# Two gated long convolutions: tables of 28 channels at once, a shift filter by matmuls on a transposed k, fixed regions instead of pools, and a new order

## The chip, the cores and the metric

The kernel runs on one core of one Trainium2 chip. The metric is the device time of one execution in microseconds (us); of several runs the median counts. A core has five engines with a queue each: PE (matmul), DVE (vector), ACT (scalar, with function tables), POOL (here index patterns) and SP (which issues most of the DMAs). Each engine works through its own queue in order, and semaphores hold an instruction until what it needs is there.

## What is computed

Two branches over L = 2048 steps and D = 448 channels are mixed by a gate. All inputs and the output are bf16.

```python
# branch A (N = 256 modes per channel)
dt = exp(log_dt); A = A_re + 1j*A_im; dB = dt*(B_re + 1j*B_im); C = C_re + 1j*C_im
K[d, l] = sum_n( C[d, n] * exp(dt[d] * A[d, n] * l) * dB[d, n] ).real
a = causal_conv(u, K) + u * Dskip                      # by FFT of length 2L in the reference
# branch B
k_shift[t] = sum_{i<4} k[t - i] * shift_k[:, i]        # 4 taps, per channel
kv = k_shift * v
b = q * (causal_conv(kv, ssm_k) + kv * ssm_D)
# mix
g = sigmoid(sum_d u[:, d] * gate_w[d])
out = g * a + (1 - g) * b
```

In this kernel's inputs u stands in for q.

## The kernel before, in words

Layout. The 448 channels are four groups of 112. An array such as u, v or k lies in SBUF with partition 32g + a for group g and slow time index a (32 of them), and with 64 fast time steps times 112 channels in the free dimension (7168 numbers to a partition). The work goes by quarters H = 0..3 of 28 channels of each group, that is 112 channels at a time.

Convolutions. Each one is a discrete Fourier transform in stages, all by matmul. `spread` (constants Wc, WcK) turns the slow index into frequencies, `transform` (constant s_W) the fast one; both leave PSUM through ACT copies into tiles `zs` of 128x3584. `swapped` makes a second copy with the real and imaginary halves exchanged, by two DMAs of 448 KB on SP. `products` multiplies both copies by the other operand's spectrum (DVE, 3584 wide). `stage_a` (constant R) and `stage_b` (constant G, 1024 matmuls of 28 columns) go back to time, with ACT copies into a tile U between them. `epilogue_B` multiplies by u, `held` keeps a result, `mix` and `epilogue_A` do the gate.

Tables. The kernel K of branch A is the costly part. For each quarter `Tables.chunk` (`levels`, `reals`) makes powers of exp(dt*A) at a few exponents: phases on DVE (80 instructions of 128x224 in the whole kernel, half of them with a quarter turn added), Sin on ACT (40 of 448), magnitudes by Exp (ACT), a multiplication of both (DVE, 36), and a copy with the sign turned (`nc.scalar.mul(..., -1.0)`, ACT, 20). From them `KGen.block(j)` builds, for each of 8 blocks of 14 channels (M = 112 modes and channels in the free dimension), two tables by repeated complex multiplication on DVE: kg_TQ (25 rows, two buffers) and kg_TP (32 rows, one buffer), with kg_P as room for the four products of each complex one. 224 matmuls `pk` of 25x32 for each block sum over the modes, ACT copies the sums to kg_S, `gather` puts them in order of time with selection matmuls (`ga_sel`, 448 in all, and 8 for Dskip), and `spread` with WcK follows.

Shift filter. k is loaded by 16 DMAs in the natural layout with a halo of three steps (`kt`, 128x67x112). For each of 8 groups of 8 steps DVE multiplies by the four taps at once (`kvt`, 128x3584), 64 identity matmuls `ps_v` of 448 columns in all add the four, ACT copies the sums back to kt, and four DVE multiplications by v make kv.

Constants. `Consts.stage_b` makes G by 8 DVE phases of 512 and 16 ACT Sin of 1024, with the mask as Sin's scale.

Buffers. A pool qp of eight slots (`NBQ = 8`) of 128x3584, pools for the natural arrays, three PSUM tiles of two banks and two of one bank for the tables. The tile framework hands out slots in turn, and makes an instruction wait until its buffer is free. ssm_k arrives per quarter in a slot of its own.

Order. The code's calls are recorded by `Listed` and `Order` (lines 119 to 150) and issued in the order of the string ORDER (lines 41 to 107), each instruction held behind the one before it on its engine. That is why every instruction shows as line 144 in the profile: one reads the groups by tile names. The recorded sequence is B0, B1, B2, A0, B3, A1, A2, A3 (kind and quarter), with a block of tables in each step (`step`), and a tail that takes the last block, the mix, and A3 in two halves.

Of the kernel before, what the change touches and what calls it, by code (L numbers as in the profile page):

```python
# [18 lines left out]
PHASE = 6.2831845 / 65536  # L19
QUARTER = 16384.0  # L20
# [5 lines left out]
NBLK = 2 * NQG  # L26
M = 8 * CB
NMODE = 896
Q_LEVELS = (4, 2, 256, 1, 512)
P_LEVELS = (8, 16, 32, 64)  # L30
NR = 16
NQ = 25
EQ_N = 2 + 3 * len(Q_LEVELS)
EP_N = 2 + 3 * len(P_LEVELS) + NR
ENT = EQ_N + EP_N
E_P0 = EQ_N
E_R = EQ_N + 2 + 3 * len(P_LEVELS)
NBQ = 8
NBH = 1

ORDER = (
# [65 lines left out]
)  # L107

def entry_of(e):
    return 2 + 3 * Q_LEVELS.index(e) if e in Q_LEVELS else EQ_N + 2 + 3 * P_LEVELS.index(e)  # L110

# [518 lines left out]
def body(  # L630
# [158 lines left out]
    def kv_cols(H):  # L789
        return lambda c: kvq[H][:, :, c]  # L790
# [205 lines left out]
```

## Time and profile before

| | before |
|---|---|
| runs | 281.84, 285.15, 285.49 us, median 285.15 |
| span of the profiled execution | 282.3 us, 12050 instructions |
| DVE busy | 261.8 us (93%), 540 instructions |
| ACT busy | 250.8 us (89%), 409 instructions |
| PE busy | 213.7 us (76%), 5387 matmuls |
| POOL busy | 12.0 us (4%), 43 instructions |
| DMA | 53380 packets, 21.34 MB; 48720 packets under 512 B |

The profiled execution's own time is its span, 282.3 us, which lies between the lowest and the middle run; the median is 2.85 us above it. The profile's slices are 40 equal parts of the span (7.06 us each), a digit being tenths of busy time. A group of instructions is named by engine, operation, out<-in tile names and shape; behind the count stand the busy time of the group, the mean ns of one, and the idle time before. Stretches by window give the busy time of PE, PEld (weight loads), DVE, ACT and POOL, the TensorE clock granted, the share of DMA and the rate.

### The profile page before, as it was taken

How to read it: one execution, taken by the hardware profiler on the slowest of the kernel's cores; microseconds unless marked ns; L12 is line 12 of the kernel's file. 1: busy time of each engine (PE TensorE's matmuls, PEld its weight loads, DVE VectorE, ACT ScalarE, POOL GpSimd, SP SyncE). 2: the span in 40 equal slices, each digit the busy share in tenths (PEclk: the TensorE clock that was granted, in tenths of full speed). 3: DMA queues.
4: the chain of work that ended last, by engine and by line, in shares of the span. 5: the costliest groups of instructions: out<-in, count | busy, mean ns of one | idle time of the engine just before them, and what ended most of it. 6: DMA issues, size and time to landing. Idle time of an engine off the chain costs nothing.

```text
span 282.3 us, 12050 instructions
## 1 busy us (share of the span) xinstructions
PE 213.7 (76%) x5387; PEld 185.9 (66%) x5387; DVE 261.8 (93%) x540; ACT 250.8 (89%) x409; POOL 12.0 (4%) x43
## 2 busy tenths in 40 slices
PE   0187673776697869888889898879899999979730
PEld 0044243776586768877779787868789887869730
DVE  8999999999999997999999999999968999987950
ACT  5999999999999999999999999999979999948500
POOL 8005000001000001000000000000000000000000
PEclk9999797565888997999999997988979999979995
DMA  6999997590501360240000070015050003430068
GB/s 116 190 182 176 158 168 105 187 175 6 135 2 19 69 115 10 73 107 2 5 2 5 6 181 0 5 22 114 9 128 2 2 5 73 112 88 5 2 126 138
DMA packets 53380, 21.34 MB, mean 76 GB/s; under 512 B 48720, under 2 KB 51664, under 8 KB 53328
## 3 DMA queue, kind: packets, MB, share of 16 engines
q1 hardware_dynamic: 48768, 19.42, 37.2%
q10 hardware_dynamic: 4560, 1.15, 2.2%
q8 instruction: 42, 0.69, 1.1%
q14 instruction: 10, 0.08, 0.1%
HBM read 10.01 MB, written 3.21 MB: 47 GB/s over the span
## 4 chain that ended last, share of the span: by engine, by line
ACT 34%; DVE 30%; PE 21%; issue 5%; DMA 3%; SPq 2%; DVEq 0%
ACT zs L144 11%; PE pk L144 8%; ACT ET L144 8%; DVE kg_P L144 7%; DVE kg_TP L144 5%; PE ps_b L144 4%; ACT zsK L144 4%; ACT U L144 4%; DVE zsS L144 3%; PE ps_c L144 3%; PE ps_a L144 3%; DVE kg_TQ L144 3%; DVE zs L144 2%; DVE kvt L144 2%; DVE ks_ph L144 2%
## 5 line engine op out<-in xcount | busy, mean ns | idle before, releaser
L144 ACT CAST zs<-ps 128x896 bf16<-128x896 f32 x48 | 44.0, 940 | 0.8 <-PE ps L144 0.7
L144 ACT CAST zs<-ps_c 128x1024 bf16<-128x1024 f32 (+1 forms) x48 | 43.4, 933 | 0.0
L144 PE MATMUL pk<-kg_TP,kg_TQ 128*25 128x32 bf16 x1792 | 33.8, 239 | 8.8 <-issue 6.6
L144 PEld LDWEIGHTS <-s_W 128*128 128x128 bf16 x544 | 31.0, 105 | 12.1 <-issue 8.7
L144 PEld LDWEIGHTS <-kg_TQ 128*25 128x25 bf16 x1792 | 28.6, 128 | 12.2 <-issue 8.2
L144 PE MATMUL ps_a<-sa_R,zs 128*128 128x128 bf16 x224 | 34.1, 239 | 3.0 <-ACT zs L144 1.3
L144 DVE TENSOR_TENSOR kg_P<-kg_TQ,ET 128x896 bf16<-128x896 bf16 (+2 forms) x56 | 35.9, 654 | 0.0
L144 PE MATMUL ps<-zs,s_W 128*128 128x112 bf16 x384 | 29.3, 231 | 7.3 <-ACT zs L144 6.2
L144 PE MATMUL ps_a<-sa_R,zsS 128*128 128x128 bf16 x224 | 33.7, 239 | 1.2 <-DVE zsS L144 1.2
L144 PEld LDWEIGHTS <-zsS 128*128 128x128 bf16 x224 | 30.1, 153 | 4.9 <-issue 3.0
L144 ACT CAST U<-ps_a 128x1024 bf16<-128x1024 f32 (+2 forms) x30 | 28.6, 959 | 5.0 <-PE ps_a L144 5.0
L144 PE MATMUL ps_b<-U,sb_G 128*128 128x28 bf16 x1024 | 28.8, 174 | 3.4 <-DVE U L144 1.2
L144 PEld LDWEIGHTS <-zs 128*128 128x128 bf16 x224 | 30.2, 152 | 1.3 <-issue 0.3
L144 PEld LDWEIGHTS <-sb_G 128*128 128x128 bf16 x1024 | 27.8, 96 | 4.3 <-issue 2.3
L144 DVE TENSOR_TENSOR kg_P<-kg_TP,ET 128x1792 bf16<-128x1792 bf16 (+1 forms) x32 | 30.6, 969 | 0.0
L144 DVE TENSOR_TENSOR kg_TQ<-kg_P 128x448 bf16<-128x448 bf16 (+2 forms) x56 | 23.1, 419 | 0.0
L144 PEld LDWEIGHTS <-scratch 128*128 128x128 bf16 x65 | 6.8, 109 | 24.6 <-issue 19.7
L144 ACT ACTIVATE ET<-ks_ph 128x448 bf16<-128x448 int16 x40 | 22.5, 604 | 0.0
L144 ACT CAST zsK<-ps_c 128x384 bf16<-128x384 f32 (+2 forms) x27 | 21.3, 797 | 0.6 <-PE ps_c L144 0.6
L144 DVE TENSOR_TENSOR kg_TP<-kg_P 128x896 bf16<-128x896 bf16 (+2 forms) x40 | 19.7, 503 | 0.2 <-PE pk L144 0.2
L144 PE MATMUL ps_c<-Wc,kv 128*64 128x128 bf16 x224 | 16.6, 303 | 3.9 <-ACT zs L144 3.6
L144 PE MATMUL ps_v<-kvt,scratch 128*128 128x448 bf16 x64 | 16.1, 405 | 4.0 <-ACT kt L144 3.2
(103 smaller groups left out, 463.3 us busy)
## 6 DMA issues: line engine op xcount, KB each, us to landing
zsS<-zs SPq DMA_DIRECT2D x16, 448.0 KB, 5.7
kt<-in_B_k_dram SPq DMA_DIRECT2D x16, 112.0 KB, 4.0
skraw<-in_B_ssm_k_dram SPq DMA_DIRECT2D x16, 112.0 KB, 5.0
vt<-in_B_v_dram SPq DMA_DIRECT2D x4, 448.0 KB, 7.7
uu<-in_A_u_dram SPq DMA_DIRECT2D x4, 448.0 KB, 8.8
xfd<-ks_hold SPq DMA_DIRECT2D x2, 672.0 KB, 3.2
ks_xf<-xfd SPq DMA_DIRECT2D x3, 336.0 KB, 3.7
out_dram<-ug SPq DMA_DIRECT2D x8, 112.0 KB, 4.0
```

The lines of the kernel that those rows point to most:

```text
L144: ins = f(*args, **kw)
```

## The change

The kernel is rewritten around the same stages.

- Tables of 28 channels at once: `M` is 224, there are four tables instead of eight, each instruction is twice as wide, and TQ, TP, ET have one region each for the whole kernel. TQ has 32 rows (21 hold table entries, the others products on their way, and the last one is zero), so a sum is a matmul of 32x32 instead of 25x32. The products are written into rows of the table that are still unused.
- Batched phases: the phases of three or four exponents lie in one tile; 40 of 224 are multiplied out, and one DVE addition per batch gives the quarter turn. Sin takes a whole batch (12 instructions of 1344 or 1792). The sign is turned on DVE.
- The filter: k is loaded transposed (channel on the partition) by four transposing DMAs on SP; 448 matmuls against diagonal matrices of the taps put the shifted sums straight into PSUM in the natural layout, and eight DVE products (128x896) from PSUM with v replace v in place.
- G: two ACT Sin of 2048 and eight DVE multiplications by the mask's columns.
- Regions: `Places` has six slots of 128x3584 and four PSUM rooms of two banks; which slot or room each use gets is read from the strings SLOTS and ROOMS. COPIES says for each of 190 evacuations whether ACT or DVE makes it (five by DVE). ssm_k has one region for all quarters; its four small additions go from POOL to DVE; u's region first holds three quarters of the transposed k.
- A swap is eight DMAs of 112 KB. Two quarters of the scaled modes stay in SBUF (`hold`), two go through DRAM.
- PLAN, and a new ORDER: T0, B0, B1, T1, B2, A0, T2, B3, A1, T3, A2, the mixes, A3, with T3's gather and A3 in halves.

The core of the diff:

```diff
-CB = NC // 2
-NBLK = 2 * NQG
-M = 8 * CB
+M = 8 * NC
...
+NSLOT = 6
+PLAN = (("T", 0), ("B", 0), ("B", 1), ("T", 1), ("B", 2), ("A", 0), ("T", 2), ("B", 3), ("A", 1), ("T", 3), ("A", 2), ("m", 0), ...
+class Places:
+    def __init__(self, pool, psum):
+        self.slots = [pool.tile([P, 3584], bf16, name="q%d" % i) for i in range(NSLOT)]
+        self.rooms = [psum.tile([P, 2, 512], f32, name="ps%d" % i) for i in range(4)]
...
     def stage_b(self, ...):
-            for g in range(4):
-                nc.scalar.activation(G[:, b0:b0 + 16, :, g, :]..., low16(ph...), ACT.Sin, scale=mask[:, g:g + 1])
+            nc.scalar.activation(tmp..., low16(ph...), ACT.Sin, scale=PHASE)
+            for g in range(4):
+                nc.vector.tensor_scalar(out=G[:, 32 * i:32 * i + 32, :, g, :]..., in0=tmp, scalar1=mask[:, g:g + 1], scalar2=None, op0=ALU.mult)
...
     def levels(self, ...):
-        for i, e in enumerate(levels):
-            unit(E[:, :, 0:2], e if e in P_LEVELS else -e, 0.0, 1)      # two phases of 224, one Sin of 448
-            V.tensor_tensor(out=E[:, :, 0:2], in0=E[:, :, 0:2], in1=mag[:, i]..., op=ALU.mult)
-                nc.scalar.mul(B[:, :, :, 2], B[:, :, :, 0], -1.0)
+        for lev in LEVELS:
+            for i, e in enumerate(lev):
+                V.tensor_scalar(out=ph[:, i, 0], in0=f, scalar1=sign * TURN, scalar2=..., op0=ALU.mult, op1=ALU.add)
+            V.tensor_scalar(out=ph[:, :, 1], in0=ph[:, :, 0], scalar1=QUARTER, scalar2=None, op0=ALU.add)
+            self.nc.scalar.activation(E[:, :, 0:2]..., low16(ph...), ACT.Sin, scale=PHASE)
+            V.tensor_tensor(out=E[:, s:, 0:2], in0=E[:, s:, 0:2], in1=E[:, s:, 2]..., op=ALU.mult)
+            V.tensor_scalar(out=E[:, :, 2], in0=E[:, :, 0], scalar1=-1.0, scalar2=None, op0=ALU.mult)
...
     def sums(self, parts):
+        for w0, w1 in parts:
+            for w in range(w0, w1):
+                for hf in range(2): for c in range(2): for g in range(4):
+                            nc.tensor.matmul(o..., lhsT=self.TQ[:, :, c, m], rhs=rhs, ..., tile_position=(0, 32 * g))
...
-    for b0 in (48, 32, 16, 0):
-        for g in range(4):
-            nc.sync.dma_start(kt[g * 32:(g + 1) * 32, 3 + b0:19 + b0, :], k4[g][:, b0:b0 + 16, :])
+    for g in range(4):
+        nc.sync.dma_start_transpose(out=kT[g][:, 64:2112], in_=B_k[0][:, COL0[g]:COL0[g] + 128])
...
-    for b0 in range(56, -1, -8):
-        V.tensor_tensor(out=t[:], in0=bass.AP(k0...), in1=wt..., op=ALU.mult)
-        for i in range(2):
-            for n in range(4):
-                nc.tensor.matmul(pt[:, i, 0:448], lhsT=ident, rhs=t[:, n, 4 * i:4 * i + 4, :]..., start=(n == 0), stop=(n == 3))
-        evac(kt[:, b0 + 3:b0 + 11, :]..., pt[:, :, 0:448])
+    for b0 in range(0, 64, 8):
+        pt = places.room()
+        for i in range(2):
+            for d in (0, -1, 1, -2, 2, -3, 3):
+                t0 = b0 + 4 * i + d
+                j0, j1 = max(0, -d), min(4, 4 - d)
+                for g in range(4):
+                    x = kT[g][:, 64 + t0:64 + t0 + 64 * 31 + 1:64]
+                    nc.tensor.matmul(pt[32 * g:32 * g + 32, i, 112 * (d + j0):112 * (d + j1)], lhsT=x,
+                                     rhs=dg[:, g, j0:j1]..., start=(d == 0), stop=(d == 3), tile_position=(0, 32 * g))
+        V.tensor_tensor(out=o, in0=pt[:, :, 0:448], in1=o, op=ALU.mult)      # o: 8 steps of v
...
     def swapped(zs):
-        for r in range(2):
-            nc.sync.dma_start(swap[64 * r:64 * r + 64], zs[64 - 64 * r:128 - 64 * r])
+        for k0 in range(0, 32, 8):
+            for r in range(2):
+                nc.sync.dma_start(swap[64 * r:64 * r + 64, k0:k0 + 8], zs[64 - 64 * r:128 - 64 * r, k0:k0 + 8])
...
     def load_sk(H):
-        nc.gpsimd.tensor_tensor(out=raw[:, :, 0], in0=raw[:, :, 0], in1=dB[:, H * NC:(H + 1) * NC], op=ALU.add)
+        V.tensor_tensor(out=skr[:, :, 0], in0=skr[:, :, 0], in1=dB[:, H * NC:(H + 1) * NC], op=ALU.add)
```

More of the change, by code (lines that the diff above doesn't have):

```diff
@@ L308, in col_of, with __init__, __call__, rows_of @@
         return self.sel[:, self.var[key]].rearrange("p a b -> p (a b)")
-def spread(nc, psum, W, zs, cols, groups, evac, room=8, tag="ps", at=0):
-    for n, whs in enumerate(groups):
-        pt = psum.tile([P, room, 128], f32, name="ps_c", tag=tag)
+class Copies:
+    def __init__(self, nc):
+        self.nc, self.n = nc, 0
+    def __call__(self, dst, src):
+        self.n += 1
+        if COPIES[self.n - 1] == "V":
+            self.nc.vector.tensor_copy(dst, src)
+        else:
+            self.nc.scalar.copy(dst, src)
+def rows_of(zs, k0, k1, c0, c1):
+    return zs[:, k0:k1, :, c0:c1].rearrange("p k g c -> p (k g) c")
+def spread(nc, places, W, zs, cols, groups, evac):
+    for whs in groups:
+        pt = places.room()[:].rearrange("p a (i n) -> p (a i) n", n=128)
         for i, wh in enumerate(whs):
@@ L373, in stage_b @@
[L373 to L386 removed]
+        evac(rows_of(zs, 0, 32, whs[0], whs[0] + m), pt[:, 0:m].rearrange("p i kg -> p kg i"))
@@ L727, in body @@
-    sk0 = load_sk(0)
-    vt = natt([P, 64, 112], "vt", "natv")
+    modes = [qt([3, 4, 256])[0:112] for _ in range(2)]
+    raw = {}
+    for i, (nm, src) in enumerate((("A_re", A_A_re), ("A_im", A_A_im), ("B_re", A_B_re), ("B_im", A_B_im), ("C_re", A_C_re), ("C_im", A_C_im))):
+        raw[nm] = modes[i // 3][:, i % 3]
+        nc.sync.dma_start(raw[nm], src.rearrange("(g l) n -> l g n", g=4))
+    taps = places.slot()[:]
+    wr = shaped(taps, [448, 4])
+    nc.scalar.dma_start(wr.rearrange("p d t -> p (d t)"), B_shift_k.rearrange("d t -> (d t)").partition_broadcast(P))
@@ L732, in body @@
-    uu = natt([P, 64, 112], "uu", "natu")
-    for g in range(4):
-        nc.sync.dma_start(uu[g * 32:(g + 1) * 32], u4[g])
     dB = wp.tile([P, 112], bf16, name="dB")
@@ L742, in body @@
     nc.sync.dma_start(d4[:], A_Dskip.rearrange("(g l) -> g l", g=4))
-    dt = kgp.tile([P, 448], bf16, name="ks_dt", tag="kg_S")
-    nc.scalar.activation(dt[:], ldt[:], ACT.Exp)
     ji = cons.carve(P)
@@ L756, in body @@
-    wt = cons.carve(224).bitcast(bf16).rearrange("p (t l) -> p t l", t=4)
-    nc.scalar.copy(wt, wraw.rearrange("p l t -> p t l")[:, ::-1])
-    for b0 in range(56, -1, -8):
-        pt = psum.tile([P, 2, 512], f32, name="ps_v", tag="ps")
-        t = qt([P, 4, 8, 112], "kvt")
-        k0 = kt[:, b0:b0 + 8, :]
-        V.tensor_tensor(out=t[:], in0=bass.AP(k0.tensor, k0.offset, [list(k0.ap[0]), [112, 4], [112, 8], [1, 112]]),
-                        in1=wt.unsqueeze(2).to_broadcast([P, 4, 8, 112]), op=ALU.mult)
-        for i in range(2):
-            for n in range(4):
-                nc.tensor.matmul(pt[:, i, 0:448], lhsT=ident, rhs=t[:, n, 4 * i:4 * i + 4, :].rearrange("p b l -> p (b l)"),
-                                 start=(n == 0), stop=(n == 3))
-        evac(kt[:, b0 + 3:b0 + 11, :].rearrange("p (i b) l -> p i (b l)", i=2), pt[:, :, 0:448])
@@ new lines, in body @@
+    nc.scalar.activation(dt, ldt, ACT.Exp)
+    a1, g1 = cons.field(0, 31), cons.field(5, 3)
+    maskg = cons.onehot(4, g1)
+    dg = shaped(taps, [4, 4, 112], at=1792)
+    for g0, g1_, sh in ((0, 3, 0), (3, 4, 16)):
+        n = g1_ - g0
+        V.tensor_tensor(out=dg[:, g0:g1_], in0=wr.rearrange("p (g l) t -> p g t l", g=4)[:, g0:g1_],
+                        in1=ident[:, sh:sh + 112].unsqueeze(1).unsqueeze(1).to_broadcast([P, n, 4, 112]), op=ALU.mult)
+    room = arena["TQ"][:]
+    Wc = cons.stage_c("Wc", a1, maskg)
@@ new lines, in body @@
+    W2 = cons.stage_2(cons.field(0, 63), [cons.field(6, 1, -QUARTER, (1 + r) * QUARTER) for r in range(2)], room)
+    R = cons.stage_a(cons.field(0, 63), [cons.field(6, 1, HALF, QUARTER), cons.field(6, 1, HALF, 0.0)])
+    cons.stage_b(G, cons.field(2, 31, 4.0, 1.0), cons.onehot(4, cons.field(0, 3)), room)
+    half = shaped(arena["TP"][:], [2, 2, 896], f32, at=3584)
+    held_back = qt([2, 3, M], f32)
+    modal = Modes(nc, places, raw, ident, dt, (hold, held_back), shaped(arena["RK"][:], [2, 896], at=896), [half[:, 0], half[:, 1]], evac)
@@ new lines, in body @@
+    uu = arena["natu"][:].rearrange("p (b l) -> p b l", l=112)
+    for g in range(4):
+        nc.sync.dma_start(uu[g * 32:(g + 1) * 32], u4[g])
+    ug = vt
+    gwt = qt([112, 32])
+    gw2 = wp.tile([P, 112, 2], bf16, name="gw2")
+    V.tensor_copy(gw2[:], gw[:].unsqueeze(2).to_broadcast([P, 112, 2]))
+    V.tensor_tensor(out=gwt.rearrange("p n (a t) -> p n a t", t=2), in0=gw2[:].unsqueeze(2).to_broadcast([P, 112, 16, 2]),
+                    in1=one[:].rearrange("p (a t) -> p a t", t=2).unsqueeze(1).to_broadcast([P, 112, 16, 2]), op=ALU.mult)
@@ new lines, in body @@
+    pg = places.room()[:, 0]
+    for l in range(112):
+        q = 32 * (l % 4)
+        nc.tensor.matmul(pg[q:q + 32, 0:64], lhsT=gwt[:, l, :], rhs=uu[:, :, l], start=(l < 4), stop=(l >= 108), tile_position=(0, q))
+    evac(gx[:, 0:64], pg[:, 0:64])
+    nc.tensor.matmul(pg[:, 128:192], lhsT=gx[:, 64:192], rhs=gx[:, 0:64], start=True, stop=True)
+    gt = wp.tile([P, 64], f32, name="gt")
+    nc.scalar.activation(gt[:], pg[:, 128:192], ACT.Tanh, scale=0.5)
+    V.tensor_scalar(out=gt[:], in0=gt[:], scalar1=0.5, scalar2=0.5, op0=ALU.mult, op1=ALU.add)
@@ L930, in body @@
-    nc.scalar.copy(gx[:, 0:64], pg[:, 0:64])
-    nc.tensor.matmul(pg[:, 128:192], lhsT=gx[:, 64:192], rhs=gx[:, 0:64], start=True, stop=True)
-    gt = wp.tile([P, 64], f32, name="gt")
-    nc.scalar.activation(gt[:], pg[:, 128:192], ACT.Tanh, scale=0.5)
-    V.tensor_scalar(out=gt[:], in0=gt[:], scalar1=0.5, scalar2=0.5, op0=ALU.mult, op1=ALU.add)
-    gb = wp.tile([P, 64, 2], bf16, name="gb")
-    V.tensor_copy(gb[:], gt[:].unsqueeze(2).to_broadcast([P, 64, 2]))
-    og = wp.tile([P, 64, 2], bf16, name="og")
@@ new lines, in table @@
+    def table(H):
+        if H >= 2:
+            nc.sync.dma_start(hold[:, H - 2], xfd[:, H - 2])
+        kg.exps(H)
+        kg.reals(H)
+        kg.levels(H)
+        kg.tables(H)
+        if H < NQG - 1:
+            kg.sums([(0, NC)])
+            kg.gather(H, 0, NC)
+            return spread_in(kg.cols, WcK)
+        kg.sums([(0, CB), (CB, NC)])
+        zs = qt([32, 4, NC])
+        for w0 in (0, CB):
+            kg.gather(H, w0, w0 + CB)
+            spread(nc, places, WcK, zs, kg.cols, [range(w0, w0 + 8), range(w0 + 8, w0 + CB)], evac)
+        return zs
@@ new lines, in mix @@
+    def mix(H):
+        o, x = window(ug, 0, 64, H), window(uu, 0, 64, H)
+        if H == NQG - 1:
+            V.tensor_tensor(out=o, in0=o, in1=x, op=ALU.mult)
+        weighed(o, og)
+        if H < NQG - 1:
+            weighed(x, gb)
+            V.tensor_tensor(out=o, in0=o, in1=x, op=ALU.add)
+    KA = {}
+    for what, H in PLAN:
+        if what == "T":
+            KA[H] = table(H)
+        elif what == "B":
+            conv_B(H)
+        elif what == "A":
+            conv_A(H, KA[H])
+        else:
+            mix(H)
```

809 lines of the change are left out of this document (341 added, 468 removed), and 128 rows, old and new, of tables (ORDER, built).

## The prediction

> **What bounds the kernel now.** I read the page's busy shares first, then the slices, then the stretches by window, then the groups by form, and last the timeline of DVE. The prices below are from this one execution.
>
> ```profile
> span 282.3 us, 12050 instructions
> PE 213.7 (76%) x5387; PEld 185.9 (66%) x5387; DVE 261.8 (93%) x540; ACT 250.8 (89%) x409; POOL 12.0 (4%) x43
> ...
> DVE  8999999999999997999999999999968999987950
> ACT  5999999999999999999999999999979999948500
> ...
> q1 hardware_dynamic: 48768, 19.42, 37.2%
> ```
>
> DVE is busy in nine tenths of nearly every slice, ACT almost as much: two engines bound the kernel together, and no wait is long. Two stretches stand out:
>
> ```profile
> 0.00:20.00 20.00, 6.52 (x33) 3.47 (x33) 19.08 (x70) 16.88 (x17) 5.70 (x39) 1.00 0.94 161
> 20.00:40.00 20.00, 14.69 (x120) 7.88 (x121) 20.00 (x37) 19.81 (x29) 3.99 (x1) 0.91 1.25 168
> ...
> 260.00:283.00 23.00, 9.26 (x266) 8.89 (x262) 12.11 (x19) 4.69 (x6) 0.00 (x0) 0.81 0.46 82
> ```
>
> In the first 40 us DVE (fourth number) has no gap although the loads saturate the queues (the last two numbers: DMA share, GB/s). At the end both engines thin out. The prices (count, total us, mean ns of one):
>
> ```profile
> L144 DVE TENSOR_TENSOR kg_P<-kg_TP,ET 128x1792 bf16<-128x1792 bf16 x24 | 25.6, 1086 | 0.0
> L144 DVE TENSOR_TENSOR kg_P<-kg_TQ,ET 128x896 bf16<-128x896 bf16 x40 | 24.5, 621 | 0.0
> L144 DVE TENSOR_TENSOR kvt<-kt,scratch 128x3584 bf16<-128x3584 bf16 x8 | 16.0, 2007 | 0.0
> L144 DVE TENSOR_SCALAR ks_ph<-ks_xf 128x224 int32<-128x224 f32 x60 | 15.2, 272 | 0.4 <-ACT ET L144 0.4
> L144 DVE TENSOR_TENSOR ug<-ps_b,uu 128x896 bf16<-128x896 f32 x6 | 6.5, 1088 | 0.0
> L144 DVE TENSOR_SCALAR s_ph<-scratch 128x1024 int32<-128x1024 int32 x4 | 3.2, 801 | 0.0
> L144 DVE TENSOR_SCALAR sa_R<-sa_R 128x256 bf16<-128x256 bf16 x1 | 0.2, 207 | 0.0
> ```
>
> ```profile
> L144 ACT ACTIVATE ET<-ks_ph 128x448 bf16<-128x448 int16 x40 | 22.5, 604 | 0.0
> L144 ACT ACTIVATE sb_G<-sb_ph,scratch 128x1024 bf16<-128x1024 int16 x16 | 17.5, 1148 | 0.0
> L144 ACT ACT_TABLE_LOAD x11 | 14.1, 1283 | 3.1 <-issue 2.9
> L144 ACT ACTIVATE ET<-ET 128x448 bf16<-128x448 bf16 x16 | 9.9, 620 | 0.0
> ```
>
> And the last table operation of DVE, with the next:
>
> ```profile
> 243.54 0.27 DVE L144 TENSOR_TENSOR kg_TQ<-kg_P 128x224 bf16<-128x224 bf16 x1
> 243.73 2.02 DVE L144 TENSOR_TENSOR zsS<-zsS,zsK 128x3584 bf16<-128x3584 bf16 x1
> ```
>
> **DVE's sum.** Means times counts give 306.4 us over 540 instructions, busy is 261.8: neighbours overlap by 44.6/540 = 83 ns, so one instruction costs its mean less 83 ns. A bf16 product costs 0.62 us at 896, 1.086 at 1792, 2.02 at 3584: the fixed part left after overlap is about 0.07 us, so fewer, larger instructions alone save little.
> - Tables: 380 instructions, 188.9 us of means, 157.5 after overlap. After: 148 products and additions (20 of 3584, 40 of 1792, 12 of 1344 at 0.85 between its neighbours, 60 of 896, 16 of 448) = 137.4; 40 phases of 224 = 10.7; 12 additions of a quarter turn = 6.5; 12 negations = 4.0; 4 copies 1.1. That is 159.7 in 216, or 141.9: -15.6. The gain is in 40 phases, and in work that merges.
> - Filter: 8 of 2007 and 4 of 1087 go (12 instructions, 19.4); 8 products from PSUM at 1088 and two for the diagonals (0.85, 0.39) come (9.1): -10.3.
> - The rest (148 before and after) goes from 84.9 to 82.1: the tables G cost 8 multiplications of 2048 (0.67 each, 5.4), against half as many phases and cheaper evacuations.
>
> DVE is then 233.0 instead of 261.8. Three forms have no row: the quarter turn (int32 to int32), the negation and G (bf16 times a scalar). I take the steeper of what rows allow: 224 int32 cost 272 and 1024 cost 801, 0.66 ns per element, so 672 would be 0.57 and 12 of them 7.2; 256 bf16 cost 207 (nearest for G and negation). At one element per 0.96 ns cycle, as the rows from PSUM run, G would cost 2.2 each: +12, and the others +12. Low end 0, high end +24; of G's, 6 of 8 lie where DVE must wait anyway, so +15 counts. I take 0.
> The Trainium skill, page "VectorE: DVE Perf Modes" (the rules for kernel authors), gives bf16 copies and scalar operations in SBUF four times the plain rate: that agrees with the 207 ns row, and by it G and negations cost what I took.
>
> **ACT's sum.** Overlap here is (300.7 - 250.8)/409 = 122 ns. The -1 products go to DVE: 20 instructions, 9.2 after overlap. G's 16 Sin (16.4) become 2 of 2048 at the s_W row's 1900 (3.6). 40 Sin of 448 (19.3) become 12 wider (15.9). Eight kt copies go (6.2 with 898 each). Table loads go from 11 to 16: +5.8. Wider evacuations save some 6. ACT: 250.8 to about 216.5.
>
> **PE** loses ps_v (64 matmuls, 16.1 us) and gets 448 matmuls of 256 columns on the mean. In before, 296 ga_sel matmuls of 112 columns in four tiles side by side took 9.1 us, 31 ns each; by columns this gives 12 to 20 us. Equal, and hidden by the start.
>
> **What the start adds.** In before k came in 16 pieces and DVE's first filter product began at 11.57 us; it never waited. Now the first filter product (76 instructions, about 30 us, stand ahead of it) needs all of the transposed k, v and 56 matmuls. Price of a packet: 37.2% of 16 x 282.3 us over 48768 packets = 34.4 ns on one of 16 engines. Before it stand modes 2688 packets (5.8 us of all 16), taps and log_dt 3.5, a quarter of ssm_k 1.9, v 8192 packets (17.6), and k. k by one packet per 256-byte row of 8192: 17.6. Sum 46.4. In before kt, modes, a quarter of ssm_k and v (48.7 by the same price) had landed by 37 us: 48.7/(37 - 1.5 of start) = 1.37 per us. So 46.4/1.37 + 1.5 = 35.4, with the matmuls 36 us, and DVE, there at 31, waits about 5.5 us. Bounds for k: by bytes at the window's 165 GB/s, 12.7 us, no gain beyond v; 128-byte pieces, 16384 packets, +12.7 us. Behind that DVE instruction stand T0's table work and the four additions on ssm_k; ACT stands at its first spread copy until 44 us with 26 us of work ahead. From there it has 190 us: 44 + 190 + 16 behind = 250, so ACT is nearly as late as DVE and hides nothing.
> No row here shows a transposing load. The Trainium skill, page "VectorE: DVE Perf Modes" (the three transpose paths), has 1309 ns for a 128x128 block; 64 blocks in a row would be 84 us, and the sum 70 us longer. The same skill, page "Advanced Engine Details and Errata" (X-Bar Transpose), has such loads as fast as others, by which the row's price holds.
>
> **Other edits.** The swaps go in 64 pieces instead of 16: 48 more issues on SP at about 0.5 us (its kt issues), where SP is idle; a piece of 112 KB lands in 4.0 us instead of 5.7, eight are issued in 4, so a swap lands at about 8 us, behind the next spread. A single TQ and TP instead of two TQ: table H+1 waits for the sums of H (448 matmuls at 33.8/1792 = 18.9 ns, 8.5 us); between them DVE has four products of 3584 and phases, about 11 us. The four additions on ssm_k move from POOL, which is idle after its first 40 index patterns, to DVE (about 0.17 us each, counted), and there wait for SP's loads. ssm_k has one region: quarter H+1 loads after the spread of H, a whole convolution ahead. Between 0 and 2 us, taken as 0; if the cover of a table is gone, up to 8.5 us for each of three.
>
> **The end.** Before, 38.6 us lie behind the last table operation (243.7 to 282.3). The new tail has 448 sums instead of 224 (+4.2) and a wider gather (+1.6), halved to overlap: +2 to +7, I take +4. DVE has 22.6 us of its 233 behind T3 and 210.4 ahead. Sum: 0.9 start + 210.4 + 5.5 + 6.4 (the stalls of before) + 38.6 + 4 = 265.8 of span against 282.3. The runs' median, 285.15, lies 1.0% above that span, so the time is near 267.
>
> **Rivals.**
> - *Transposed k arrives late* (0.24, slower). Every us after 36 moves the end by one. It decides (285) when k takes 31 us instead of 12.8, which is 19,700 packets or pieces of about 106 bytes. With 64-byte pieces (32768 packets, 51 us) the time is 267 + 38 = 305. For: every other load moves small pieces at a price per packet. Against: rows of 256 bytes lie together in memory.
> - *Unseen forms at one element per cycle, or bare table buffers* (0.13, no change). +15 on DVE, or two of three 8.5-us covers gone: 281 to 283.
> - *The new order is fuller* (0.13, faster). The stalls of 6.4 and the start's 5.5 are absorbed, tail +2: 254.
>
> **How the numbers follow.** Forecast 267, chance 0.50, own range 258 to 276. A difference under 2% (279.4 to 290.9) can't be told from none. Faster: 0.50 + 0.13 = 0.63; same 0.13; slower 0.24. The range 252 to 299 leaves out about 0.15 at the late end and 0.05 at the low one.
>
> **What would show it.** DVE busy near 233 in 374 instructions, ACT near 217; one DVE wait of 3 to 10 us before the first product from PSUM, ended by v or PE; G at 0.67 us; phase sums at 0.5 to 0.6; behind the last table operation 41 to 46 us. Wrong would be: the first filter matmul later than 45 us, DVE busy above 250, or PE sums releasing DVE for over 5 us a table.

## The result, and the profile after

| | before | after |
|---|---|---|
| median of the runs on one chip | 283.50 us (4 runs, 281.28 to 285.49) | 293.79 us (4 runs, 292.38 to 296.11) |
| ratio after/before | | 1.036, 95% interval 1.027 to 1.044 |
| span of the profiled execution | 282.3 us | 291.0 us |
| last table operation of DVE ends at | 243.8 us | 240.3 us |
| stretch behind it | 38.5 us | 50.7 us |
| PE idle up to the end of the filter, its first work | 18.7 us | 23.5 us |

The changed kernel is slower by 3.6%, where 267 us and a gain were forecast. (The 285.15 us that the forecast started from is the median of three of these four runs of before.) Run again beside 14 runs of before (e15 below) it had 293.56 against 286.47, a ratio of 1.025 (1.021 to 1.029): its median is steady, that of before lay between 283.5 and 286.5 in six groups of runs, so the loss is 2.5 to 3.6%. Below, a kernel made from after is held against 293.8 or 293.6, one made from before against the before of its own runs, and differences of 1 us are taken as none. Because the groups differ, the size of a small gain of a kernel made from after is known only to about 2 us: taken as ratios to the before of their own runs, against e15's 1.025, the gains of e2, e5 and e13 below come out at about 2 us each instead of 3.6 to 3.9, e3's at 12.4 instead of 14.8 and e14's at 10.6 instead of 12.2. The page of after (busy us, share of the span, instructions; then tenths in 40 slices of 7.3 us; then a DMA queue with its packets, MB and share; then the shares of the chain that ended last):

```profile
span 291.0 us, 12305 instructions
...
PE 219.8 (76%) x5599; PEld 203.9 (70%) x5599; DVE 242.2 (83%) x374; ACT 224.3 (77%) x322; POOL 9.9 (3%) x53
...
PE   0155786878796998997699988687998967899820
...
DVE  8869999999997699999789997893999985524950
ACT  3378949799887889999779899993999994268600
...
q8 instruction: 44, 0.72, 1.0%
...
PE 35%; ACT 27%; DVE 22%; issue 7%; DMA 5%; POOL 0%; SPq 0%; ACTq 0%; DVEq 0%; POOLq 0%
```

DVE has 20 us less to do and ACT 26 us less, 68 and 77% of what was forecast, and the time rose all the same. In before both rows showed nines almost throughout; now no row does, and PE has taken the first place in the chain of what ended last (in before that chain was 34% ACT, 30% DVE and 21% PE). The work saved has become idle time. Four stretches of 40 us from the middle show how evenly (after; the columns are the length of the stretch, busy time of PE, PEld, DVE, ACT and POOL with instructions, granted clock, DMA share, GB/s):

```profile
80.00:120.00 40.00, 35.19 (x1008) 32.89 (x997) 35.57 (x51) 34.97 (x52) 0.00 (x0) 0.87 0.23 49
120.00:160.00 40.00, 34.52 (x945) 31.90 (x945) 36.12 (x50) 35.94 (x51) 0.00 (x0) 0.96 0.24 55
160.00:200.00 40.00, 33.31 (x925) 30.77 (x923) 35.10 (x44) 34.95 (x56) 0.00 (x0) 1.00 0.21 49
200.00:240.00 40.00, 35.50 (x749) 33.43 (x750) 36.30 (x46) 38.13 (x56) 0.00 (x0) 0.91 0.07 17
```

PE, DVE and ACT are each busy for 83 to 95% of every stretch: three queues in balance, none of them full. Such a page cannot say which of the three holds the other two. The waits of PE in after (releaser: us in all, times, longest) give a first hint:

```profile
PE ps L135 <- ACT q L135: 19.1, 48, 1.3
PE ps L135 <- DMA q<-in_A_B_re_dram: 13.5, 1, 13.5
PE ps L135 <- issue: 10.2, 9, 2.6
PE ps L135 <- DVE natv L135: 6.4, 3, 3.2
```

and against them the one line of that view in before that has the same releaser as the third:

```profile
PE pk L144 <- issue: 6.6, 6, 2.4
```

"issue" means that PE waited for no semaphore that the profile shows; what it waited for is found in e9 below. In after eight of the nine pauses, 9.9 of the 10.2 us, stand before sums of the tables, of which the change puts 448 in a row instead of 224.

PE's ledger of the span, before to after: busy 213.7 to 219.8 (+6.1), idle up to the end of the filter 18.7 to 23.5 (+4.8), issue pauses 7.2 to 10.2 (+3.0), all other waits 31.1 to 24.5 (-6.6), behind the last matmul 11.6 to 13.0 (+1.4). Sum +8.7, which is 291.0 - 282.3. What PE's own work gained, by stage (its timeline added up): spread with WcK 9.7 to 15.6, filter 16.2 to 18.9, stage_a 35.0 to 36.4, against gather 9.7 to 7.6, the smaller spread 9.8 to 8.3 and the others within 1.2. The biggest of these was in no step of the prediction. Groups of PE (count, busy us, mean ns of one), in before

```profile
L144 PE MATMUL ps_c<-WcK,kg_KT 128*64 128x128 bf16 x224 | 12.0, 231 | 2.1 <-ACT zsK L144 1.9
L144 PE MATMUL ps_c<-Wc,kv 128*64 128x128 bf16 x224 | 16.6, 303 | 3.9 <-ACT zs L144 3.6 <-DVE kv L144 0.3
```

and in after:

```profile
L135 PE MATMUL ps<-WcK,RK 128*64 128x128 bf16 x224 | 16.4, 296 | 1.4 <-DVE natv L135 0.6 <-ACT RK L135 0.4 <-issue 0.3
L135 PE MATMUL ps<-Wc,natv 128*64 128x128 bf16 x224 | 16.1, 293 | 4.0 <-DVE natv L135 2.6 <-ACT q L135 1.3
```

The same 224 matmuls take 296 ns each instead of 231. The kernel table KT is now stored as [8, 8, 28], so the 64 numbers of a weight column lie 56 bytes apart; the spread of v, whose weights have always been strided, shows 303 in before and 293 in after.

At the start nothing went wrong for DVE. Its timeline of after, and the one wait of more than 1 us that it has before 40 us:

```profile
36.65 2.07 DVE L135 TENSOR_TENSOR natv<-ps,natv 128x896 bf16<-128x896 f32 x2
```

```profile
DVE Wc L135 <- ACT TP L135: 3.4, 1, 3.4
```

The first filter product runs at 36.65 us with no idle time noted before it: 90 instructions stand ahead of it, 32.0 us of work, and 4.7 us of waits in all. The transposing loads of k whose landing is recorded came 4.4 to 4.9 us after their issue, the last at 25.5 us; the last load of v landed at 35.4.

The end is what has grown. PE's timeline behind DVE's last table operation (start, us, instruction, idle before it), and three lines of DVE's, the last table operation first:

```profile
240.70 2.54 PE L135 MATMUL ps<-TP,TQ 128*32 128x32 bf16 x139 [0.25 <-ACT q L135]
243.99 2.37 PE L135 MATMUL ps<-TP,TQ 128*32 128x32 bf16 x128 [0.74 <-issue]
247.99 1.34 PE L135 MATMUL ps<-TP,TQ 128*32 128x32 bf16 x69 [1.63 <-issue]
```

```profile
239.16 1.16 DVE L135 TENSOR_TENSOR TQ<-TQ,ET 128x896 bf16<-128x896 bf16 x2
...
249.02 3.96 DVE L135 TENSOR_TENSOR q<-q,q 128x3584 bf16<-128x3584 bf16 x2 [4.70 <-DMA q<-q]
260.00 0.62 DVE L135 CAST q<-ps 128x448 bf16<-128x448 f32 x1 [7.01 <-PE ps L135]
```

DVE waits here for a swap and for PE. PE is busy for 32.8 us behind the last table operation, against 23.7 in before: twice the sums, and what else had not been got through by then.

### The profile page after: what moved, and what is told of

The parts are those of the page before. It is cut to its first block, busy times and chain, and to the rows that moved or that the text cites. A ratio compares the mean times of both kernels' runs of the same rounds, so it can differ in the third digit from the quotient of the medians.

```text
span 291.0 us, 12305 instructions
## 1 busy us (share of the span) xinstructions
PE 219.8 (76%) x5599; PEld 203.9 (70%) x5599; DVE 242.2 (83%) x374; ACT 224.3 (77%) x322; POOL 9.9 (3%) x53
## 4 chain that ended last, share of the span: by engine, by line
PE 35%; ACT 27%; DVE 22%; issue 7%; DMA 5%; POOL 0%; SPq 0%; ACTq 0%; DVEq 0%; POOLq 0%
PE ps L135 35%; ACT q L135 20%; DVE TP L135 6%; DVE TQ L135 4%; ACT RK L135 4%; DVE natv L135 3%; DMA q<-in_A_C_im_dram 2%; DVE q L135 2%; DMA q<-in_A_B_re_dram 2%; ACT ET L135 2%; DVE PH L135 1%; DVE ET L135 1%; DVE G L135 1%; ACT natu L135 1%; DVE RK L135 1%
## 5 line engine op out<-in xcount | busy, mean ns | idle before, releaser
L135 ACT CAST q<-ps 128x1024 bf16<-128x1024 f32 (+4 forms) x160 | 135.2, 937 | 8.5 <-PE ps L135 8.1
L135 PEld LDWEIGHTS <-q 128*128 128x128 bf16 (+2 forms) x720 | 56.0, 149 | 18.1 <-DMA q<-in_A_B_re_dram 13.5
L135 DVE TENSOR_TENSOR TQ<-TQ,ET 128x896 bf16<-128x896 bf16 (+1 forms) x56 | 44.6, 818 | 0.0
L135 PE MATMUL ps<-q,s_W 128*128 128x112 bf16 (+1 forms) x544 | 36.2, 221 | 10.9 <-ACT q L135 10.8
L135 PE MATMUL ps<-TP,TQ 128*32 128x32 bf16 x1792 | 32.8, 242 | 11.2 <-issue 9.9
L135 DVE TENSOR_TENSOR q<-q,q 128x3584 bf16<-128x3584 bf16 (+1 forms) x22 | 32.4, 1509 | 10.3 <-DMA q<-q 4.7
L135 PEld LDWEIGHTS <-TQ 128*32 128x32 bf16 x1792 | 30.7, 155 | 13.3 <-issue 12.3
L135 PEld LDWEIGHTS <-natu 128*32 128x32 bf16 (+1 forms) x560 | 30.4, 182 | 11.8 <-DMA natu<-in_B_k_dram 6.0
L135 PE MATMUL ps<-sa_R,q 128*128 128x128 bf16 x448 | 37.8, 250 | 1.0 <-ACT q L135 0.7
L135 DVE TENSOR_TENSOR TP<-TP,ET 128x3584 bf16<-128x3584 bf16 (+2 forms) x20 | 30.7, 1552 | 0.0
L135 PEld LDWEIGHTS <-G 128*128 128x128 bf16 x1024 | 27.2, 97 | 3.3 <-issue 2.6
L135 PE MATMUL ps<-q,natu 128*32 128x224 bf16 (+3 forms) x336 | 18.9, 332 | 8.7 <-DMA natu<-in_B_k_dram 5.4
L135 ACT ACT_TABLE_LOAD x16 | 20.5, 1283 | 2.0 <-PEq L915 1.7
L135 PEld LDWEIGHTS <-natv 128*64 128x64 bf16 x224 | 15.6, 212 | 4.4 <-DVE natv L135 2.7
```

Of the source, the lines that this page charges most:

```text
L135: ins = f(*args, **kw)
```

## The experiments

Four theories were set against each other, and the expectations call them by letter. A: no engine binds, each waits for the others in turn, so that taking work from any one of them gives little. B: DVE still binds, as the prediction had it. C: PE's queue, worked off in order, holds the time, its issue pauses included. D: the order alternates stretches that only PE fills with stretches that only ACT fills. In the diffs, `nc.skip()` records a call that is not issued. Medians of before measured together with each group of runs stand with them.

**One engine relieved at a time (before: 285.98 us in the same runs).**

e1, DVE without the eight `back` products of 3584:

```diff
-        self.nc.vector.tensor_tensor(out=T[:, 16 + i0:16 + i1]..., in0=src, in1=self.R[:, i0:i1]..., op=ALU.mult)
+        self.nc.skip()
...
-  rhs = bass.AP(r0.tensor, r0.offset, [list(r0.ap[0]), [32 * M + (1 - 2 * c) * M, 2], [2 * M, 16]])
+  rhs = bass.AP(r0.tensor, r0.offset, [list(r0.ap[0]), [(1 - 2 * c) * M, 2], [2 * M, 16]])
```

> The changed kernel without the eight products that build the upper half of TP (8 of 128x3584 at 2.018 us, 15.5 us of DVE after overlap); the sums then read the lower half twice, with as many matmuls, so the kernel K is not the right one. Theory A (no engine bounds any more; PE, ACT and DVE hand the work to each other and each waits for the others): the time falls by 3 to 8 us, and DVE's idle time grows by the rest. Theory B (DVE is still the bound, as the prediction had it): 13 to 16 us less. Theory C (PE is the new bound): 0 to 3 us less.

Measured: 293.26 us, against 293.79. The page of e1:

```profile
PE 217.4 (75%) x5599; PEld 201.7 (69%) x5599; DVE 227.0 (78%) x366; ACT 224.2 (77%) x322; POOL 9.9 (3%) x53
```

DVE's busy time fell from 242.2 to 227.0 us and the time did not move: DVE alone does not bind after, and B falls.

e2, ACT without 45 of its 64 Exp of the real powers:

```diff
         for i in range(NR):
+            if i and H:
+                self.nc.skip()
+                continue
             self.nc.scalar.activation(...)
```

> The changed kernel without 45 of the 64 Exp of 128x224 that make the decays for the upper half of TP (15 in each of tables 1, 2, 3; 45 x (410 - 122) ns = 13 us of ACT), so those tables hold old values. Theory A (all three engines wait for each other): 2 to 6 us less. Theory B (DVE bounds): 0 to 3 us less. Theory C (PE bounds): 0 to 3 us less. If ACT were the bound: 11 to 13 us less.

Measured: 289.9 us, -3.9 for 11 us of ACT. ACT is partly on the path; A had said 2 to 6, C 0 to 3, which it misses by a little.

e3, PE with half of the sums:

```diff
                         for g in range(4):
+                            if hf:
+                                nc.skip()
+                                continue
...
-  start=(hf == 0 and c == 0), stop=(hf == 1 and c == 1)
+  start=(c == 0), stop=(c == 1)
```

> The changed kernel with half of the sums over the modes: 896 matmuls of 32x32 instead of 1792 (32.8/2 = 16.4 us of PE), so K is summed over half the modes. Theory A (all three wait for each other): 5 to 10 us less, part of it the 4 us of table 3 in the tail. Theory B (DVE bounds): the tail's 4 us less. Theory C (PE bounds): 14 to 17 us less.

Measured: 278.95 us, -14.8; to before 0.981 (0.970 to 0.993). The page and PE's issue pauses of this kernel:

```profile
span 276.3 us, 10513 instructions
...
PE 201.4 (73%) x4703; PEld 186.3 (67%) x4703; DVE 241.8 (88%) x374; ACT 223.9 (81%) x322; POOL 9.9 (4%) x53
```

```profile
PE ps L142 <- issue: 1.3, 2, 0.9
```

18.4 us of PE's work and 8.9 us of pauses are gone, and the slower kernel becomes faster than before, with DVE and ACT as busy as they were. Of these 27 us 12 do not come through, mostly because PE then waits longer for ACT (19.1 to 27.2 us by the same release, `ACT q`). C's forecast is met.

e4, before without its sixteen `back` products (the same edit as e1):

> The control: the kernel before without the same products (16 of 128x1792 at 1086 ns, 16 us of DVE), the sums reading the lower half twice. The reading that DVE bounds the kernel before gives 12 to 16 us less; if ACT, busy 89%, takes over at once, 5 to 9 us less.

Measured: 285.62 against 285.98, ratio 1.000 (0.994 to 1.007). So DVE alone did not bind in before either, at 93% of the span.

**The same two questions to before, and two layouts (before: 285.04 us).**

e6, before with half of the sums (the edit of e3):

> The kernel before with half of the sums over the modes (896 matmuls of 25x32 instead of 1792, 33.8/2 = 16.9 us of PE; K is summed over half the modes). Theory C (TensorE's queue holds the time in the kernel before as well): 10 to 16 us less. If ACT holds it: 0 to 4 us less.

Measured: 278.84, -6.2; ratio 0.977 (0.971 to 0.984). e7, before without 45 Exp (the edit of e2):

> The kernel before without 45 of its 64 Exp of 128x224 for the decays of the upper half of TP (13 us of ACT; quarters 1 to 3 hold old values there). Theory C: 0 to 4 us less. If ACT, busy 89%, holds the time of the kernel before: 9 to 13 us less.

Measured: 285.48, ratio 1.003 (0.999 to 1.006), nothing. In before too, of the three only PE moves the time, but less than half as far as in after, and C's 10 to 16 us for e6 is missed. e3 and e6 end at the same 279. What holds them there was not tried; in the chain that ended last ACT comes first, with 35% in e3 and 55% in e6. DVE and ACT relieved at once, which e16 does to after, was not tried on before.

e5, after with KT stored so that a weight column is contiguous. All work is kept:

```diff
-  self.S, self.KT = shaped(arena["RK"][:], [32, NC]), shaped(arena["RK"][:], [8, 8, NC], at=32 * NC)
+  self.S, self.KT = shaped(arena["RK"][:], [32, NC]), shaped(arena["RK"][:], [NC, 8, 8], at=32 * NC)
...
-  self.evac(KT[:, :, r + 1 - per:r + 1, w0:w1], room.rearrange("p r (b n) -> p b r n", b=8))
+  self.evac(KT[:, w0:w1, :, r + 1 - per:r + 1], room.rearrange("p r (b n) -> p n b r", b=8))
...
-  return self.KT[:, :, :, c].rearrange("p b r -> p (b r)")
+  return self.KT[:, c].rearrange("p b r -> p (b r)")
```

> The changed kernel with the gathered K stored channel by channel (28x64, as the kernel before had it), so that the weights of the spread with WcK are 64 adjacent numbers instead of 64 at a stride of 56 bytes. In the traces the 224 matmuls of that spread take 15.6 us after the change and 9.7 before. Theory C (TensorE's queue holds the time in both kernels, and the change gave it work): 4 to 6 us less, TensorE busy about 6 less. Theory A (three engines wait for each other): 1 to 3 us less. Theory B (DVE bounds): no change.

Measured: 290.24, -3.6. The group of these matmuls in e5:

```profile
L135 PE MATMUL ps<-WcK,RK 128*64 128x128 bf16 x224 | 9.5, 233 | 1.8 <-DVE natv L135 1.0 <-ACT RK L135 0.4 <-issue 0.3
```

Back at 233 ns, and the stage from 15.6 to 8.7 us. At most about half of the 6.9 us comes through to the time; PE's issue pauses grew to 12.2 us and its waits for `ACT q` from 19.1 to 21.8. The forecasts of C (4 to 6) and A (1 to 3) lie on both sides. That this layout is one cost of the change is shown by e11 and e12 below, which differ in it alone within one group of runs.

e8, before with v's product stored channel by channel, so that the weights of its spread are contiguous too:

```diff
-            pair = qt([P, 2, 64, NC], "kv")
+            pair = qt([P, 2, NC, 64], "kv")
...
-        V.tensor_tensor(out=kvq[H], in0=q(vt[:]), in1=q(kt[:, 3:67]), op=ALU.mult)
+        V.tensor_tensor(out=kvq[H].rearrange("p c b -> p b c"), in0=q(vt[:]), in1=q(kt[:, 3:67]), op=ALU.mult)
```

> The kernel before with kv stored channel by channel (28x64), so that the weights of its spread (224 matmuls, 16.6 us or 70 ns each from start to start) are adjacent numbers, as those of ssm_k are (43 ns each). PE: 224 x 27 ns = 6 us less; the four DVE products that write kv get a stride, at most 4 us more on DVE. Theory C: 2 to 6 us less, 0 to 2 of them lost where the first kv product stands in the way at 40 us. Theory B (DVE bounds): 0 to 4 us more.

Measured: 313.44, +28 us (ratio 1.099, 1.091 to 1.107). The products in e8:

```profile
L144 DVE TENSOR_TENSOR kv<-vt,kt 128x1792 bf16<-128x1792 bf16 x4 | 32.2, 8255 | 0.8 <-ACT kt L144 0.8
```

They took 1085 ns each before. PE's spreads did fall, from 31.4 to 26.8 us, but a DVE output whose neighbouring numbers go 128 bytes apart costs far more, which no theory had. In e5 ACT writes a channel-by-channel layout at no cost (931 ns a copy of 896 numbers in after, 933 in e5), but in runs of four or more adjacent numbers; the two patterns are not the same.

**The pauses, the start and the order (before: 285.89 us).**

e9 runs the 448 sums of the first table three times in a row, so that the pauses can be seen by themselves:

```diff
+            if not nc.extra:
+                nc.extra = 2 * nc.calls[-448:]     # issued ahead of the first table's own sums
```

> The changed kernel with the 448 sums of table 0 made three times in a row (896 matmuls of 32x32 more; two passes are thrown away). In its trace PE stood still 9 times, 10 us in all, each time within or just behind a run of sums and 128 matmuls apart. If these pauses belong to long runs of short matmuls as such, the 1344 matmuls take 1344 x 18.3 ns = 24.6 us and about ten pauses more, together 33 to 42 us, one pause for each 128. If they come from something else that happened to fall there (transfers, a wait that is not shown), 25 to 28 us.

Measured: 319.98 us (one run), 26.2 more than after, or 29 ns for each added sum. The 1344 matmuls ran from 83.9 to 123.2 us, 39.3 us with 32 others among them: the pauses belong to the runs of sums. PE's timeline in these sums:

```profile
91.17 2.17 PE L142 MATMUL ps<-TP,TQ 128*32 128x32 bf16 x128 [2.39 <-issue]
95.17 2.18 PE L142 MATMUL ps<-TP,TQ 128*32 128x32 bf16 x128 [1.83 <-issue]
98.62 2.19 PE L142 MATMUL ps<-TP,TQ 128*32 128x32 bf16 x128 [1.28 <-issue]
102.35 2.20 PE L142 MATMUL ps<-TP,TQ 128*32 128x32 bf16 x128 [1.53 <-issue]
105.81 2.18 PE L142 MATMUL ps<-TP,TQ 128*32 128x32 bf16 x128 [1.26 <-issue]
```

A pause after every 128 matmuls, each with its weight load, that is after every 256 instructions. Eight such starts from 91.17 to 116.99 give 25.82/7 = 3.69 us for 128, or 28.8 ns a sum where the matmuls alone take 2.18 us, 17 ns. The profile also shows what PE waits for. Its DMA table has a queue q8 of the kind "instruction", in the page of after 44 packets with 0.72 MB, 16384 bytes each. In e9, from 91 to 117 us, it had:

```profile
q8 instruction: 7, 0.11, 1.7%
```

That is one packet for each block of 128 sums, and 16384/256 = 64 bytes for an instruction. The count fits the whole kernel too: 44 packets of 256 are 11264, and PE has 11198 matmuls and weight loads in after. In the traces these pauses end shortly after such a packet has landed: 1.3 to 1.5 us after it in all nine of after, 1.3 to 1.6 in all seven of before, and 1.2 to 1.6 in 19 of the 20 of e9. For example the packet that landed at 93.59 us is followed by the start at 95.17, the one at 97.08 by the start at 98.62. PE was waiting for its next instructions: 128 such sums are worked off in 2.2 us, and a new packet came every 3.7.

e10, the filter with one tap of four:

```diff
                 for g in range(4):
+                    if d:
+                        nc.skip()
+                        continue
```

> The changed kernel with one tap of the filter instead of four (64 of the 448 filter matmuls, so k_shift is not the filtered k). PE: the filter takes 18.9 us in the trace, 384 of 448 matmuls go, about 14 us less. Theory C in its simple form (every us on TensorE's queue counts): 10 to 14 us less. If the start is held by the loads and DVE's 36 us of work ahead of the filter's first product: 0 to 2 us less.

Measured: 293.56 us, nothing, with 384 matmuls fewer (PE 211.8 us busy). This is a miss for C in its simple form: at the start PE's work is covered, as the prediction said, here by the loads of v and by DVE's work ahead of the filter's first product, and its queue can hold the time only from there on.

e11 (D's test) keeps every instruction of after and gives them a new order from 50 us on, planned with the durations and the pauses of the traces (ORDER and ROOMS are other strings). e12 is that order with e5's KT.

> The changed kernel with the same instructions in another order from 50 us on (other PSUM rooms accordingly): the sums of a table and the copies to PSUM-bound stages are set side by side, planned with the durations of this trace. Theory D (the order alternates stretches in which PE works and ACT waits, the sums, with stretches in which ACT works and PE waits, the transforms; the saved work of DVE and ACT cannot be used): 6 to 12 us less, with ACT's waits for sums cut and DVE busy over 90% from 50 us on. Theory C in its simple form (PE's work is the time): 0 to 3 us less, since PE has the same work.

> The same new order, and K stored channel by channel as in the fifth experiment. Theory D: 279 to 283 us, below both kernels, and DVE the bound (242 us of work, 1 us ahead, about 13 behind, under 15 us of gaps). Theory C: the 3.6 us of the fifth experiment and no more, 289 to 291 us.

Measured: 292.88 (-0.9) and 287.75 (286.57 to 290.45), the latter 1.008 of before (1.004 to 1.012), the best whole version of the changed kernel and still not below before. The forecast of 279 to 283 for e12 failed, and D mostly with it; C's 289 to 291 is missed on the other side. Between e11 and e12 KT's layout alone is worth 5.1 us, with intervals that do not touch (1.017 to 1.032 and 1.004 to 1.012 of before). As for D, DVE gets to its last table operation at 236.3 in both, and then the end takes 54.4 and 49.2 us. The waits of DVE in e12 begin with

```profile
DVE q L146 <- PE ps L146: 15.4, 1, 15.4
```

which is PE working through sums, gather and the stages of A2 that the order had put off. Moving DVE ahead moved PE's work behind it.

**DVE and ACT at once (before: 286.47 us).** DVE and ACT, each of little effect alone, could still hold the time together. e16 makes the edits of e1 and e2 both; e15 is after unchanged, in the same runs.

> The changed kernel as it is, in the same runs as e16, because its median of 293.79 stands beside a before of 283.50 and the later groups had before at 285.0 to 286.0: differences of one or two us between groups are not told apart by it. Every theory expects a ratio to before between 1.027 and 1.044, about 293 to 295 us.

> The edits of e1 and e2 together on the changed kernel: DVE without the eight products of back (sums read the lower half of the table twice) and ACT without 45 of its 64 Exp; DVE falls by 15 us of busy time, ACT by 11, PE keeps all its work. If PE's queue paces the kernel (C), the two together give little more than e2 alone: 288 to 290. If DVE and ACT hold each other up in turn and each only hid the other's gain (A), relieving both at once gives much more than the sum of e1 and e2: 280 to 283.

Measured: 293.56 and 289.2. With 15 us of DVE and 11 us of ACT taken away together the gain is 4.4 us, that of e2 alone (3.9) within what can be told. A falls for after, and with it the reading that DVE and ACT together bind it. Nor is it the clock: the granted clock was 0.88 to 0.91 in the runs of e15 and 0.88 to 0.90 in those of before beside them.

**Middle or end (before: 285.77 us).** Left open so far was whether the widened last table costs more than the others, because its sums stand alone at the end. e13 leaves half of the sums out in T3 alone, e14 in T0 to T2 alone:

```diff
+        short = len(parts) > 1      # e13: T3; e14: len(parts) == 1, T0 to T2
...
+                            if hf and short:
+                                nc.skip()
+                                continue
```

> The changed kernel without half of the sums of the last table T3 alone (hf 1 left out: 224 of its 448 matmuls, so only half of the rows of the tables goes into that sum; all else stays). Taking half of the sums of all four tables away gave 14.8 us. If the queue of PE holds the time evenly over the whole span, a table is worth a quarter of that: -3.7 us, 290.1. If the end is a chain of its own, in which the sums of the widened last table stand with nothing beside them, each left-out matmul counts with its pause, 224 at 28.8 ns: -6.4, about 287.4, and the stretch behind the last table operation of DVE shortens from 50.7 to about 44. If the end is held by ACT's copies or by the swaps, nothing: 293.8.

> The complement: half of the sums of T0, T1 and T2 left out (672 matmuls), those of T3 complete. Evenly held by PE's queue: -11.1 us, 282.7, with the last table operation of DVE near 230 instead of 240.3 and the stretch behind it unchanged at 50.7. If the end is a chain of its own that was worth 6.4: -8.4, 285.4. If the two do not add up to 14.8, the freed time in the middle is partly taken by DVE or ACT before the end.

Measured: 289.86 (-3.9) and 281.56 (-12.2). The page of e14:

```profile
span 279.1 us, 10961 instructions
...
PE 206.4 (74%) x4927; PEld 190.7 (68%) x4927; DVE 241.9 (87%) x374; ACT 223.8 (80%) x322; POOL 9.9 (4%) x53
```

Per matmul left out that is 3.9/224 = 17 ns at the end and 12.2/672 = 18 ns in the middle (e3: 14.8/896 = 17): evenly held within what can be told, and the end as a chain of its own with a price of 28.8 ns falls. In e14 DVE's last table operation

```profile
229.26 1.15 DVE L142 TENSOR_TENSOR TQ<-TQ,ET 128x896 bf16<-128x896 bf16 x2
```

ends at 230.4 us, 9.9 earlier, though DVE's work was not touched, and the stretch behind it is 48.7 us; in e13 it comes at 242.1 and the stretch behind it is 45.9 instead of 50.7. So PE paces DVE in the middle. That the end is long because PE arrives there with work in arrears is the reading of these numbers; no run tried it by itself.

## Why the prediction was wrong

- **What bounds the kernel: wrong, and this is the step that failed.** "Two engines bound the kernel together" was read from busy shares of 93% and 89%. Taking DVE work (e4) or ACT work (e7) out of before gave nothing, taking sums from PE, at 76%, gave 6.2 us (e6). In after 15 us of DVE gave nothing (e1), DVE and ACT together 4.4 (e16), half of PE's sums 14.8 (e3). Both at once were not taken out of before, so there it is shown only that neither holds the time alone. A busy share tells how long an engine worked, not what the span would do if it worked less.
- **DVE's sum: 233 forecast, 242.2 measured**, in the 374 instructions counted. The forms without a row came near what was taken:

```profile
L135 DVE TENSOR_SCALAR G<-TQ,TP 128x2048 bf16<-128x2048 bf16 x8 | 5.9, 742 | 0.0
L135 DVE TENSOR_SCALAR PH<-PH 128x672 int32<-128x672 int32 x8 | 4.9, 617 | 0.0
...
L135 DVE TENSOR_SCALAR ET<-ET 128x672 bf16<-128x672 bf16 x8 | 3.1, 386 | 0.0
```

  G at 742 ns (0.67 forecast), the quarter turn at 617 (0.54), the negation at 386 (0.33): 2.0 us of the 9. That rival falls. The Trainium skill, page "VectorE: DVE Perf Modes" (Rules for kernel authors), gives such bf16 scalar operations four times the plain rate; the 742 ns for 2048 numbers agree. Another 2.2 us is overlap, 77 ns an instruction instead of 83, and 0.9 the two products for the diagonals (1549 and 617 ns for 0.85 and 0.39). ACT was 224.3 for 217. The sums were good enough; e1 shows that they were sums of the wrong engine.
- **Slips in the sums, none of them decisive.** ACT's listed terms add up to 219.0, not 216.5. 265.8 raised by 1.0% is 268.5, not 267. The rows from PSUM run at 1.03 ns a number ((1088 - 625)/448, with `ept<-ps_b,gt` at 625 for 448), not 0.96. Filter matmuls priced by columns from 31 ns for 112 would take 31 us, not 12 to 20; the 18.9 measured are 42 ns each.
- **PE "equal, and hidden by the start": half right.** The filter took 18.9 us, within the 12 to 20, and hidden it was (e10). But the step looked at the filter alone. The strided KT (+5.9, of which e5 gives 3.6 of time) and the longer runs of sums (+3.0 of pauses) were put at nothing, although the page of before had the line of the pauses, and the spread of v beside that of KT showed the price of strided weights (303 against 231 ns).
- **The start: the loads right, the rest by luck, and the effect wrong.** The loads were to be there at 35.4 us, and the last of v landed at 35.4; the first product was to come at 36 and came at 36.65. The rival of late transposed loads fell: 4.4 to 4.9 us a load. The Trainium skill, page "Advanced Engine Details and Errata" (X-Bar Transpose), which has them as fast as others, agrees; the estimate of 84 us worked out from the price for a block on "VectorE: DVE Perf Modes" does not. DVE's wait of 5.5 us before the product did not come: 90 instructions stood ahead of it instead of 76, and with 32.0 us of work and 4.7 of other waits DVE reached it 1.2 us after v. So DVE and not the loads came last, and that the product still ran at the forecast time is luck. PE idles 4.8 us more up to the filter's end; whether that counts in the time was not tried by itself.
- **The other waits at 0 to 2 us:** DVE waits 3.7 us for the sums to leave TQ and 4.7 for a swap, once each; the forecast missed by far more.
- **The end: 4 us more forecast, 12.2 measured**, and ahead of it 20.5 less forecast, 3.5 measured. The runs put both down to one cause: DVE was not the pace-maker, so its saving did not bring the end nearer, and PE's sums count on both sides of the last table operation (e13, e14).
- **The rivals:** none of the three happened. The right one, that PE would take over the bound, was not among them; the range held the time only because it reached out for another rival.

What stays open: how the 8.7 us divide exactly. Shown are 2 to 5 us for KT (3.6 in e5, 5.1 from e11 to e12), nothing for the filter's extra matmuls (e10), and that PE's time is worth about 17 ns per sum left out anywhere (e13, e14). The pauses' 3.0 and the start's 4.8 us are read from the ledger and not taken away singly, and -6.6 of other waits stands against them. So the engine is shown, and of its added work only KT's part.

## What to carry to other kernels

When three engines stand at 76, 89 and 93%, ask each of them by an experiment that takes work from it alone before costing a change: here the least busy of them moved the time most. The likely reason, argued and not shown, is that its in-order queue serves both of the others. Cost a change on every engine that feeds the one it relieves, the layout of PE's weights and the length of its runs of small matmuls included; where an engine waits for no semaphore, look at the DMA queue that brings its instructions. And try the end of a kernel apart before blaming it: that the last table, batched twice as wide, costs more there than elsewhere was tried (e13) and not borne out.

## What the runs showed of the hardware

- 128 short matmuls with their weight loads (128x32 weights, 32 columns) in a row took 3.69 us, of which 2.18 busy, with a pause after every 128 (e9). Each pause ended 1.2 to 1.6 us after a packet of 16384 bytes had landed on the queue of kind "instruction" (35 of 36 pauses in before, after and e9): PE had run out of instructions. With 224 sums to a table instead of 448 the pauses nearly vanished in after (10.2 to 1.3 us in e3); before, with runs of 224 and weights of 25 columns, has 6.6 us of them.
- 64-column weights whose numbers lie 56 bytes apart cost 70 ns a matmul in the stage's time (15.6 us/224), contiguous ones 43 in before and 39 in e5 (8.7/224).
- A DVE product of 1792 bf16 numbers with neighbouring output numbers 128 bytes apart took 8255 ns instead of 1085, 4.6 ns a number (e8).
- int32 additions on DVE took 617 ns for 672 numbers and for 896 alike; 224 float to int32 took 268.
